# Moving the pair copies of q and k one slot ahead of their transposes, and software-pipelining the first unit, in a block-sparse attention kernel with a gated feed-forward layer

## The chip, the cores and the metric

The kernel runs on one core of one Trainium2 chip. The metric is the device time of one execution in microseconds (us), lower is better. Every run is marked fast or slow by its granted TensorE clock and its time; one single execution of this study was slow and is left out of all comparisons (it is shown, because it is odd).

Words used below: **PE** is TensorE, **DVE** is VectorE, **ACT** is ScalarE, **POOL** is GpSimd, whose queue issues the input loads. A **unit** is 256 query rows of one batch (12 units: 4 batches of 3). A main-loop unit has six **slots** of two steps; slots 1 and 2 carry output-layer products of an earlier unit ("output slots"), slots 3 to 6 carry gate and value products ("gated slots").

## The reference, cut to what matters

```python
scores = (1/sqrt(D)) * q @ k.T                  # B=4, H=8, S=768, D=64, float32
scores = where(mask, scores, -1e9)              # block mask of 32x32 blocks
attn = softmax(scores); x = attn @ v
x = x.transpose(0, 2, 1, 3).reshape(B*S, H*D)   # 3072 x 512
out = ((sigmoid(x @ w_gate) * (x @ w_val)) @ w_out).astype(float32)   # 512 -> 1536 -> 512
```

## The kernel before

q, k and v are loaded as float16 with the rows on partitions. A pair of heads is prepared by a DVE copy that lays the two heads side by side (`pr`), PE transposes into PSUM (`tpq`), and a copy into `qT` or `kT`:

```python
def prep(src, dst, b, p, t0=0, t1=NT, eng=None):
    pr = work.tile([128, NT, 2, D], f16, tag="pr", bufs=3, name="pr")
    nc.vector.tensor_copy(pr[:, t0:t1, :, :], src[b % 2][...])          # cut
    tp = ps.tile([128, 1024], f16, tag="m", bufs=4, name="tpq")
    for t in range(t0, t1):
        nc.tensor.transpose(tp[:, ...], pr[:, t, :, :], ident)          # cut
    # copy tp to dst[b % 2][:, p, ...] on nc.vector, or nc.scalar if asked

def vcopy(b, p): ...          # DVE: v16 -> vex (v with a column of ones), one pair

class Step:                   # one pair of heads, two key tiles, 256 queries
    def qk(self): ...         # PE: 4 matmuls -> st (PSUM, 2 buffers)
    def exp(self): ...        # ACT: pt = exp(st / 8), 128 x 1024
    def mul(self): ...        # DVE: pt *= mask
```

In the first unit each step runs to its end before the next begins; in the main loop one preparation stands at the end of a slot:

```python
for p in range(NP):                              # first unit
    for j in range(3):
        st = steps[p][j]
        st.qk(); st.exp()
        # ... build mask tiles ...
        st.mul()
        if p + 1 < NP:
            if j == 0: prep(k16, kT, 0, p + 1)
            if j == 1: prep(q16, qT, 0, p + 1, 0, 2)
        # ... xts, vcopy, value, rest of q ...

for n in range(1, len(units)):                   # main loop
    for sl in range(6):
        sa.qk(); sb.qk()                         # sb later in two slots of unit 2
        sa.exp(); sa.mul()
        F.f(fs[0])                               # gated slot; F.y(...) in an output slot
        sb.exp(); sb.mul()
        if sl % 3 in (0, 2): value()             # PV and normalisation of an earlier pair
        F.f(fs[1]); F.f(fs[2])
        if sl % 3 in (0, 1): xts()
        extra()      # one of: prep of k, prep of q, vcopy, for the next batch
```

`F.f` is 8 matmuls into `pg`, a tanh on ACT (`th`) and a product on DVE (`ht`). Program order is the order on each engine.

The softmax here doesn't subtract the row's maximum and nothing guards it: scores larger than these inputs give would overflow.

## Time and profile before

| | before |
|---|---|
| median time (4 runs) | 368.56 us (368.24 to 369.45) |
| span of the profiled run | 367.5 us |
| first scores of unit 1 / of unit 2 | 8.0 / 47.35 us |
| unit without preparations (e.g. 190.86 to 213.94) | 23.1 us |
| two units with 8 preparations (132.65 to 190.86) | 58.2 us |

First the page of the profile: busy time by engine; then the span in 40 slices of 9.2 us (a digit is the busy share in tenths; PEclk is the granted TensorE clock; GB/s is what the transfers moved); then the chain of waits that ended last, by engine.

```profile
span 367.5 us, 8103 instructions
...
PE 311.2 (85%) x3470; PEld 221.2 (60%) x3470; DVE 225.0 (61%) x534; ACT 210.9 (57%) x320; POOL 25.9 (7%) x37
...
PE   2566457889879999888889999799889999999995
...
PEclk9999999999999999999999999999999999999999
...
GB/s 108 193 202 205 204 204 181 2 3 57 2 78 162 78 2 59 2 2 58 2 2 57 3 30 30 0 2 59 3 2 57 3 30 30 2 59 1 30 30 57
...
PE 79%; DVE 11%; ACT 6%; issue 2%; DMA 1%; DVEq 0%; ACTq 0%; POOLq 0%
...
```

PE is the bound: 85% busy and 79% of the chain. But its digits show a weak start (2 to 7 for seven slices) and dents afterwards. The GB/s row shows the input transfers running at about 204 GB/s until the seventh slice, that is until about 64 us.

The dents. The view of two stretches (length, then busy time of PE, its weight loads, DVE, ACT and POOL, each with the instruction count, then the granted clock, DMA share and GB/s):

```profile
...
132.65:190.86 58.21, 50.25 (x594) 36.64 (x594) 38.60 (x92) 34.43 (x52) 0.00 (x0) 1.00 0.05 20
190.86:213.94 23.08, 23.08 (x273) 16.97 (x272) 15.86 (x38) 17.00 (x26) 0.00 (x0) 1.00 0.07 24
...
```

In units without preparations PE never stops. In the two units with eight of them it is idle for 58.21 - 50.25 = 8.0 us. The tile view of `tpq` in this stretch gives just that: 8 waits for the copy `pr`, 8.0 us in total. One of them in order of time (start, duration, engine, line, operation, output <- input, count, and in brackets the engine's idle time before it and what ended it):

```profile
...
150.60 0.87 DVE L303 SCALAR_TENSOR_TENSOR ht<-th,pg 128x256 f16<-128x256 f32 x2
150.63 0.38 ACT L302 ACTIVATE th<-pg 128x256 f32<-128x256 f32 x1 [0.49 <-PE pg L292]
151.38 0.28 DVE L279 COPY xT<-tpx 128x256 f16<-128x256 f16 x1
151.58 0.35 DVE L188 COPY pr<-k 128x768 f16<-128x768 f16 x1
...
151.99 0.51 PE L194 MATMUL tpq<-ident,pr 128*128 128x128 f16 x6 [1.29 <-DVE pr L188]
...
152.43 0.61 PE L222 MATMUL st<-qT,kT 64*128 64x256 f16 x8
...
```

DVE works off its queue in order: the last two `ht` of the slot, then xT, then `pr`; the input of this copy was on chip since about 64 us, when the loads of the first three batches were done. The transposes wait 1.29 us for the copy, and the scores (L222), which need nothing of it, wait behind the transposes. This agrees with the Trainium skill, "TensorE: Matmul & The Clock Gate", the specification table, which calls DVE's queue a strict FIFO.

The first unit, one step in order of time:

```profile
...
29.11 0.69 DVE L236 TENSOR_TENSOR pt<-pt,mask 128x1024 f16<-128x1024 f16 x1 [0.71 <-ACT pt L232]
29.72 0.35 DVE L188 COPY pr<-k 128x768 f16<-128x768 f16 x1
...
30.13 0.82 PE L194 MATMUL tpq<-ident,pr 128*128 128x128 f16 x6 [1.91 <-DVE pr L188]
...
32.20 0.61 PE L222 MATMUL st<-qT,kT 64*128 64x256 f16 x4
...
32.85 1.02 ACT L232 ACTIVATE pt<-st 128x1024 f16<-128x1024 f32 x1 [3.29 <-PE st L222]
...
```

Product, copy, transposes (PE waited 1.91 us), PV, scores, exponential (ACT waited 3.29 us): one serial chain through three engines.

And the clock. The same eight score matmuls early and late:

```profile
...
57.18 1.04 PE L222 MATMUL st<-qT,kT 64*128 64x256 f16 x8
...
64.81 0.61 PE L222 MATMUL st<-qT,kT 64*128 64x256 f16 x8
...
```

Until 61.4 us every matmul of this run ran at half rate. The PEclk row prints 9 there because the trace has no clock record before that time; the durations decide. The Trainium skill, "TensorE: Matmul & The Clock Gate", Part 1, describes it: half clock until a busy window of about 3.4 us.

### The profile page before, as it was taken

How to read it: one execution, taken by the hardware profiler on the slowest of the kernel's cores; microseconds unless marked ns; L12 is line 12 of the kernel's file. 1: busy time of each engine (PE TensorE's matmuls, PEld its weight loads, DVE VectorE, ACT ScalarE, POOL GpSimd, SP SyncE). 2: the span in 40 equal slices, each digit the busy share in tenths (PEclk: the TensorE clock that was granted, in tenths of full speed). 3: DMA queues.
4: the chain of work that ended last, by engine and by line, in shares of the span. 5: the costliest groups of instructions: out<-in, count | busy, mean ns of one | idle time of the engine just before them, and what ended most of it. 6: DMA issues, size and time to landing. Idle time of an engine off the chain costs nothing.

```text
span 367.5 us, 8103 instructions
## 1 busy us (share of the span) xinstructions
PE 311.2 (85%) x3470; PEld 221.2 (60%) x3470; DVE 225.0 (61%) x534; ACT 210.9 (57%) x320; POOL 25.9 (7%) x37
## 2 busy tenths in 40 slices
PE   2566457889879999888889999799889999999995
PEld 1133235765756866665666866566666858768682
DVE  2654455765765776775775766765775766757340
ACT  2244433655646766655566856565657867768241
POOL 8832010000010000000000000000000000000000
PEclk9999999999999999999999999999999999999999
DMA  8999999001059401001001000001001000010001
GB/s 108 193 202 205 204 204 181 2 3 57 2 78 162 78 2 59 2 2 58 2 2 57 3 30 30 0 2 59 3 2 57 3 30 30 2 59 1 30 30 57
DMA packets 23215, 21.03 MB, mean 57 GB/s; under 512 B 2164, under 2 KB 20108, under 8 KB 23180
## 3 DMA queue, kind: packets, MB, share of 16 engines
q0 software_dynamic: 19472, 14.16, 26.1%
q1 hardware_dynamic: 3708, 6.37, 4.7%
q8 instruction: 27, 0.44, 0.5%
q14 instruction: 8, 0.07, 0.1%
HBM read 28.39 MB, written 6.29 MB: 94 GB/s over the span
## 4 chain that ended last, share of the span: by engine, by line
PE 79%; DVE 11%; ACT 6%; issue 2%; DMA 1%; DVEq 0%; ACTq 0%; POOLq 0%
PE pg L292 32%; PE py L320 17%; PE st L222 11%; PE pv L254 10%; PE tpq L194 5%; ACT pt L232 5%; DVE pt L236 3%; DVE pr L188 3%; DVE ht L303 2%; DVE xT L279 1%; PE tpx L276 1%; DMA k<-in_k_dram 1%; ACT th L302 1%; PE pm L170 0%; DVE mask L182 0%
## 5 line engine op out<-in xcount | busy, mean ns | idle before, releaser
L232 ACT ACTIVATE pt<-st 128x1024 f16<-128x1024 f32 x144 | 144.7, 1021 | 66.5 <-PE st L222 65.8
L236 DVE TENSOR_TENSOR pt<-pt,mask 128x1024 f16<-128x1024 f16 x144 | 99.7, 692 | 79.0 <-ACT pt L232 78.6
L292 PE MATMUL pg<-xT,wg 128*128 128x256 f16 x576 | 87.3, 274 | 0.0
L292 PE MATMUL pg<-xT,wv 128*128 128x256 f16 x576 | 86.9, 274 | 0.0
L302 ACT ACTIVATE th<-pg 128x256 f32<-128x256 f32 x144 | 55.4, 385 | 44.0 <-PE pg L292 42.4
L320 PE MATMUL py<-wo,ht 128*128 128x512 f16 x288 | 67.7, 380 | 0.0
L303 DVE SCALAR_TENSOR_TENSOR ht<-th,pg 128x256 f16<-128x256 f32 x144 | 58.9, 416 | 11.1 <-ACT th L302 9.9
L194 PE MATMUL tpq<-ident,pr 128*128 128x128 f16 x192 | 19.8, 245 | 49.4 <-DVE pr L188 48.6
L292 PEld LDWEIGHTS <-wv 128*128 128x128 f16 x576 | 56.6, 98 | 6.7
L292 PEld LDWEIGHTS <-wg 128*128 128x128 f16 x576 | 50.7, 98 | 14.7 <-issue 8.2
L222 PE MATMUL st<-qT,kT 64*128 64x256 f16 x576 | 48.9, 288 | 0.5 <-ACT qT L199 0.5
L254 PEld LDWEIGHTS <-pt 128*128 128x128 f16 x1152 | 46.0, 102 | 4.6 <-issue 0.8
L254 PE MATMUL pv<-vex,pt 128*128 128x65 f16 x1152 | 48.0, 199 | 0.4 <-DVE pt L236 0.4
L194 PEld LDWEIGHTS <-pr 128*128 128x128 f16 x192 | 12.4, 107 | 58.7 <-DVE pr L188 57.6
L320 PEld LDWEIGHTS <-ht 128*128 128x128 f16 x288 | 25.8, 98 | 30.5 <-issue 4.2
L329 ACT ACTIVATE ysb<-py 128x512 f32<-128x512 f32 x24 | 14.3, 597 | 36.6 <-PE py L320 36.6
L222 PEld LDWEIGHTS <-kT 64*128 64x128 f16 x576 | 22.4, 96 | 14.0 <-issue 7.3
L266 DVE TENSOR_TENSOR x<-pv,rz 128x256 f16<-128x256 f32 x48 | 20.4, 424 | 1.7
L279 DVE COPY xT<-tpx 128x256 f16<-128x256 f16 x48 | 13.8, 287 | 11.7 <-PE tpx L276 11.7
L201 DVE COPY qT<-tpq 128x768 f16<-128x768 f16 (+2 forms) x19 | 9.3, 488 | 11.5 <-PE tpq L194 11.5
L201 DVE COPY kT<-tpq 128x768 f16<-128x768 f16 x16 | 8.9, 558 | 11.2 <-PE tpq L194 11.2
L276 PE MATMUL tpx<-ident,x 128*128 128x128 f16 x96 | 13.7, 226 | 1.6 <-DVE x L266 1.5
(29 smaller groups left out, 79.7 us busy)
## 6 DMA issues: line engine op xcount, KB each, us to landing
out_dram<-ysb SPq DMA_DIRECT2D x24, 256.0 KB, 2.0
k<-in_k_dram POOLq DMA_DIRECT2D x3, 768.0 KB, 19.0
q<-in_q_dram POOLq DMA_DIRECT2D x3, 768.0 KB, 9.1
v<-in_v_dram POOLq DMA_DIRECT2D x3, 768.0 KB, 11.5
wg<-in_moe_w_gate_dram POOLq DMA_DIRECT2D x4, 384.0 KB, 12.2
wv<-in_moe_w_val_dram POOLq DMA_DIRECT2D x4, 384.0 KB, 13.4
wo<-in_moe_w_out_dram POOLq DMA_DIRECT2D x3, 512.0 KB, 16.6
k<-in_k_dram POOLq DMA_DIRECT2D x4, 192.0 KB, 6.3
```

What stands on the lines that cost most here:

```text
L194: nc.tensor.transpose(tp[:, (t - t0) * 128 : (t - t0 + 1) * 128], pr[:, t, :, :], ident)
L201: nc.vector.tensor_copy(d_, tp[:, 0 : (t1 - t0) * 128])
L222: nc.tensor.matmul(self.st[:, a, i, :], kT[b % 2][o : o + D, p, t * 128 : (t + 1) * 128], qT[b % 2][o : o + D, p, u * UQ : (u + 1) * UQ], ...
L232: nc.scalar.activation(self.pt, self.st, AF.Exp, bias=0.0, scale=SCALE)
L236: nc.vector.tensor_tensor(self.pt, self.pt, m.unsqueeze(1).broadcast_to([128, 2, 2, UQ]), op=ALU.mult,)
L254: nc.tensor.matmul(self.acc[:, s, a, :], self.steps[t // 2].pt[:, a, t % 2, s * 128 : (s + 1) * 128], vex[self.b % 2][:, 2 * self.p + a, t ...
L266: nc.vector.tensor_tensor(self.x16, self.acc[:, :, :, 0:D], rz.broadcast_to([128, 2, 2, D]), op=ALU.mult,)
L279: nc.vector.tensor_copy(self.xT[:, self.p, :], tp[:, 0:UQ])
L292: nc.tensor.matmul(self.pg[:, i, :], w[:, c, f * 128 : (f + 1) * 128], self.xT[:, c, :], start=(c == 0), stop=(c == 3),)
L302: nc.scalar.activation(th, self.pg[:, 0, :], AF.Tanh, bias=0.0, scale=0.5)
L303: nc.vector.scalar_tensor_tensor(self.ht[:, f, :], in0=th, scalar=1.0, in1=self.pg[:, 1, :], op0=ALU.add, op1=ALU.mult,)
L320: nc.tensor.matmul(self.py, self.ht[:, f, s * 128 : (s + 1) * 128], wo[:, f, :], start=(f == 0), stop=(f == NF - 1),)
```

## The change

Its intent: let other work of PE stand between a pair's copy and its transposes, and run the first unit as a software pipeline, so that scores, exponentials, mask products and the next pair's transposes overlap. The core of the diff:

```diff
-    def prep(src, dst, b, p, t0=0, t1=NT, eng=None):
-        pr = work.tile([128, NT, 2, D], f16, tag="pr", bufs=3, name="pr")
+    def pair_copy(src, b, p, t0=0, t1=NT):
+        pr = work.tile([128, NT, 2, D], f16, tag="pr", bufs=4, name="pr")
         nc.vector.tensor_copy(...)
+        return pr
+    def pair_turn(pr, dst, b, p, t0=0, t1=NT, eng=None):
         tp = ps.tile(...)            # transposes and copy out, as before
...
-    def extra():
-        if todo: todo.popleft()()
+    def extra_pe():
+        if copied:
+            pr, dst, b, p, t0, t1 = copied.popleft()
+            pair_turn(pr, dst, b, p, t0, t1)
+            if dst is qT and t0 == 0:
+                vcopy(b, p)
+    def extra_copy():
+        if pairs:
+            src, dst, b, p, t0, t1 = pairs.popleft()
+            copied.append((pair_copy(src, b, p, t0, t1), dst, b, p, t0, t1))
...          # first unit, s = 0 .. 11, p, j = s // 3, s % 3:
+        if j == 0 and p + 1 < NP:
+            pair_turn(prk, kT, 0, p + 1)
+            prq = pair_copy(q16, 0, p + 1, 0, 2)
+        if s > 0: flat[s - 1].mul()
+        if s + 1 < 12: flat[s + 1].exp()
+        if j == 1 and p + 1 < NP:
+            pair_turn(prq, qT, 0, p + 1, 0, 2, nc.scalar)
+        if s + 2 < 12: flat[s + 2].qk()
...          # mask tiles, vcopy, value, xts, rest of q, cut
...          # main loop:
             sa.exp()
+            extra_pe()
             sa.mul()
...
                 xts()
-            extra()
+            extra_copy()
```

The arithmetic stays the same. The V copy no longer has a slot of its own: it follows the transposes of q in the same slot. So the eight preparations of a batch take eight slots in a row instead of eight of twelve. The new first unit bundles more than the pipeline: q's copy out of PSUM moves from DVE to ACT for the later pairs (`nc.scalar` above), and the mask tiles are built in another order.

More of the change, by code (lines that the diff above doesn't have):

```diff
@@ L335, in y @@
                 )
-    todo = deque()
-    def extra():
-        if todo:
-            todo.popleft()()
+    pairs = deque()
+    copied = deque()
+    def extra_pe():
[8 more added lines that the diff above has]
+            copied.append((pair_copy(src, b, p, t0, t1), dst, b, p, t0, t1))
     units = [(b, u) for b in range(B) for u in range(NU)]
@@ L357, in begin @@
             for p in range(NP):
-                todo.append(lambda b=b, p=p: prep(k16, kT, b + 1, p))
-                todo.append(lambda b=b, p=p: prep(q16, qT, b + 1, p))
-                todo.append(lambda b=b, p=p: vcopy(b + 1, p))
+                for src, dst in ((k16, kT), (q16, qT)):
+                    pairs.append((src, dst, b + 1, p, 0, NT))
         return [[Step(b, u, p, j) for j in range(3)] for p in range(NP)]
@@ L375 @@
     steps = begin(0)
-    prep(k16, kT, 0, 0)
-    prep(q16, qT, 0, 0, 0, 2, nc.scalar)
-    mask_blocks()
-    for p in range(NP):
-        for j in range(3):
-            st = steps[p][j]
-            st.qk()
-            st.exp()
-            if p == 0 and j == 0:
-                mask_rows()
-            if p == 0:
-                mask_tile(0, UQ, 2 * j, nc.vector)
-            if 1 <= p <= 2:
-                mask_tile(UQ, S, 3 * (p - 1) + j, nc.scalar)
-            st.mul()
-            if p + 1 < NP:
-                if j == 0:
-                    prep(k16, kT, 0, p + 1)
-                if j == 1:
-                    prep(q16, qT, 0, p + 1, 0, 2)
-            if j == 1:
-                xts()
-            if j == 0:
-                vcopy(0, p)
-                value()
-            if p == NP - 1:
-                prep(q16, qT, 0, j, 2, NT)
-        waiting.append(Pair(*units[0], p, steps[p], xTs[0]))
@@ L404 @@
-    todo.append(lambda: prep(q16, qT, 0, 3, 2, NT))
+    flat = [st for p in range(NP) for st in steps[p]]
+    pr = pair_copy(k16, 0, 0)
+    pair_turn(pr, kT, 0, 0)
+    pr = pair_copy(q16, 0, 0, 0, 2)
+    pair_turn(pr, qT, 0, 0, 0, 2, nc.scalar)
+    mask_blocks()
+    flat[0].qk()
+    flat[0].exp()
+    flat[1].qk()
+    mask_rows()
+    prk = pair_copy(k16, 0, 1)
+    mask_tile(0, UQ, 0, nc.vector)
+    prq = None
+    for s in range(12):
+        p, j = s // 3, s % 3
+        if j == 0 and p + 1 < NP:
+            pair_turn(prk, kT, 0, p + 1)
+            prq = pair_copy(q16, 0, p + 1, 0, 2)
+        if s > 0:
+            flat[s - 1].mul()
+        if s + 1 < 12:
+            flat[s + 1].exp()
+        if j == 1 and p + 1 < NP:
+            pair_turn(prq, qT, 0, p + 1, 0, 2, nc.scalar)
+        if s + 2 < 12:
+            flat[s + 2].qk()
+        if p == 0 and j < 2:
+            mask_tile(0, UQ, 2 * j + 2, nc.vector)
+        if j == 0:
+            vcopy(0, p)
+        if s >= 4 and j == 1:
+            value()
+        if s >= 6 and j == 0:
+            xts()
+        if j == 2 and p + 2 < NP:
+            prk = pair_copy(k16, 0, p + 2)
+        if 3 <= s < 9:
+            mask_tile(UQ, S, s - 3, nc.scalar)
+        if s >= 8:
+            extra_pe()
+        if 7 <= s:
+            extra_copy()
+        if s == 6:
+            for i in range(NP):
+                pairs.append((q16, qT, 0, i, 2, NT))
+        if j == 2:
+            waiting.append(Pair(*units[0], p, steps[p], xTs[0]))
@@ L406 @@
+    flat[11].mul()
+    extra_pe()
     for n in range(1, len(units)):
@@ L415 @@
             sa.exp()
+            extra_pe()
             sa.mul()
@@ L441 @@
                 xts()
-            extra()
+            extra_copy()
             for p, j in pair:
```

## The prediction

> **What bounds the kernel now.** Tensor work, plus waits at the pair copies. The chain of waits is 79% PE, 11% VectorE, 6% ScalarE. From the timeline (starts of each slot's scores):
>
> - Units without transposes of q and k take 23.1 us; those with them (second and third of a batch) 29.1 us. Per batch that is 8 preparations: 8 x 0.44 us of transposes and about 8.0 us in which PE waits for the copy `pr` (0.65 us behind slots of output work, 1.2 to 1.4 us behind gated slots, where the copy stands behind the last `ht` on VectorE). The tile view of `tpq` gives 24.2 us of such waits after 64 us.
> - The first unit runs from 7.5 to 47.35 us, a serial chain of score, exponential, mask product, pair copy, transpose; PE waits 21.3 us for `pr` in it. I estimate about 25 us of work for each engine there.
> - Until 61.4 us every matmul runs at half rate: 8 score matmuls take 1.04 us, later 0.61. This agrees with the Trainium skill, "TensorE: Matmul & The Clock Gate", Part 1 (half clock until a busy window of about 3.4 us; here PE is continuously busy from 58.15 us).
> - Input transfers run at about 204 GB/s until 64 us. From issue and time to landing, k of batch 1 lands at about 45.6, q at 49.4, v at 53.3 us.
>
> **What the change does.** Work stays the same. (a) Main loop: the copy still ends a slot, but its transposes stand behind the next slot's eight score matmuls, so 0.54 us of PE work fills the wait. VectorE is first in, first out (same page, the specification table), and the copy still waits for the last `ht`; so the wait shrinks, not vanishes: 1.2 to 1.4 becomes 0.7 to 0.85, 0.65 becomes 0.1. (b) The V copy (0.35 us) moves ahead of a mask product; the second exponential, behind the tanh, hides it. (c) The first unit issues scores two steps ahead, products one step late.
>
> **On the critical path.**
> - Batches 2 and 3: waits 8.0 to about 3.4 us each; saves about 9.7 together.
> - Batch 1 after the third slot of the second unit: about 6 us (one preparation less there, waits from about 8.2 to 3.1).
> - First unit: my hand schedule ends it at about 39 us instead of 47.4. But the second unit then meets the transfers: the k copy waits for 45.6, q for 49.4, and the V copy, now inside the third slot ahead of the mask product, for 53.3. So of 8.4 us about 6.3 remain at the end of that slot. This gate also forgives some error in my schedule.
>
> Sum 22 us: 368.5 to about 347 us, range 342 to 353. Chance of faster by over 2%: 0.95; within 2%: 0.04; slower by over 2%: 0.01.
>
> **What would show it.** Second unit's first score at 37 to 42 us; VectorE idle before the copies of k, q and v of batch 1, released by DMA; units with transposes at about 26.6 us instead of 29.1; PE waits for `pr` after 64 us falling from 24 to about 10 us; units without transposes unchanged at 23.1 us; full PE clock from about 54 us.
>
> **What would make it wrong.** PE reaching full clock much earlier in the denser first unit (faster, though the transfers cap it); VectorE, with the extra V copy, becoming the limit in gated slots (saves less); in-order waits in the first unit, such as the normalisation behind PV behind the ScalarE transpose copy, holding it beyond 43 us; batch 1 landing later than now.

## The result, and the profile after

| | before | after |
|---|---|---|
| median (4 runs each) | 368.56 us | 344.62 us (344.28 to 344.92) |
| ratio, 95% interval | | 0.9346, 0.9327 to 0.9366 |
| span of the profiled run | 367.5 us | 343.1 us |
| first scores of unit 2 | 47.35 us | 36.54 us |
| two units with 8 preparations | 58.2 us | 52.7 us |
| unit without preparations | 23.1 us | 23.1 us |

A ratio here is the mean time of one kernel's fast runs over the mean of the other's of the same rounds, so it is not quite the ratio of the medians. The same lines of the page of the kernel after:

```profile
span 343.1 us, 8102 instructions
...
PE 308.3 (90%) x3470; PEld 221.2 (64%) x3470; DVE 220.4 (64%) x531; ACT 210.3 (61%) x323; POOL 26.0 (8%) x37
...
PE   2788459899999999899999998999999999999995
...
GB/s 98 187 202 204 206 204 204 88 3 172 168 31 32 3 31 32 2 32 33 0 32 33 2 61 2 2 32 33 0 60 6 2 61 2 31 34 3 61 2 61
...
PE 76%; DMA 12%; DVE 6%; ACT 2%; POOL 2%; issue 1%; POOLq 0%
...
```

PE is 90% busy. Its row stands at 7 and 8 through the first unit (second to fourth slice of 8.6 us each), then drops to 4 and 5 for two slices, in which the transfers still run at 206 and 204 GB/s. DMA has appeared in the chain of waits with 12%: it held 1% before. The two stretches that correspond to those shown of before:

```profile
...
119.23:171.97 52.74, 49.39 (x593) 36.62 (x593) 38.30 (x93) 34.00 (x52) 0.00 (x0) 1.00 0.06 21
171.97:195.06 23.09, 23.09 (x273) 16.98 (x273) 15.59 (x37) 17.00 (x26) 0.00 (x0) 1.00 0.07 25
...
```

PE's idle time in the two units with preparations is 52.74 - 49.39 = 3.35 us, from 8.0 us; the unit without them is unchanged. (PE's busy time fell by 0.86 us as well, although the matmuls are the same. A likely reason, not tested: the record of a matmul of 256 columns is some 274 ns long while the next one starts about 110 ns after it, so each stop of PE may let one such overhang show as busy time, and there are fewer stops.) The tile view of `tpq` counts four waits for `pr` in this stretch, 2.9 us in total, where it counted eight. One preparation in order of time:

```profile
...
136.94 0.86 DVE L306 SCALAR_TENSOR_TENSOR ht<-th,pg 128x256 f16<-128x256 f32 x2
136.97 0.38 ACT L305 ACTIVATE th<-pg 128x256 f32<-128x256 f32 x1 [0.49 <-PE pg L295]
...
136.98 0.61 PE L225 MATMUL st<-qT,kT 64*128 64x256 f16 x8
...
137.73 0.28 DVE L282 COPY xT<-tpx 128x256 f16<-128x256 f16 x1
137.93 0.35 DVE L188 COPY pr<-q 128x768 f16<-128x768 f16 x1
...
138.33 0.51 PE L197 MATMUL tpq<-ident,pr 128*128 128x128 f16 x6 [0.74 <-DVE pr L188]
```

The DVE order is the same: `ht`, `ht`, xT, `pr`. But PE has run the scores (136.98 to 137.59) meanwhile, so its wait is 0.74 us instead of 1.29.

The second unit, where the chain now runs through the transfers:

```profile
...
45.56 0.36 DVE L188 COPY pr<-k 128x768 f16<-128x768 f16 x1 [5.17 <-DMA k<-in_k_dram]
...
45.97 0.82 PE L197 MATMUL tpq<-ident,pr 128*128 128x128 f16 x6 [6.19 <-DVE pr L188]
...
49.45 0.36 DVE L188 COPY pr<-q 128x768 f16<-128x768 f16 x1
...
49.87 0.82 PE L197 MATMUL tpq<-ident,pr 128*128 128x128 f16 x6 [0.80 <-DVE pr L188]
...
53.28 0.37 DVE L207 COPY vex<-v 128x768 f16<-128x768 f16 x1 [1.99 <-DMA v<-in_v_dram]
...
```

The copy of k of batch 1 stood 5.17 us on its load, and PE 6.19 us on the copy. The chain of waits in order of time names the load of q that follows (start, duration, what):

```profile
...
28.55 20.88 DMA q<-in_q_dram
...
49.45 0.37 DVE pr L188
...
49.87 0.82 PE tpq L197 x6
...
```

Where the 24.4 us of span came from, by the same event in both traces: the last gate product of unit 2's third slot ends at 63.16 us before and 55.99 us after, so **7.2 us** were won by there. Unit 4 begins at 109.55 and 96.14 us: 13.4 us, so **6.2 us** more in the rest of batch 1's preparations. Batches 2 and 3 give 58.2 - 52.7 = **5.5 us** each. Nothing changes after that.

### The profile page after: what moved, and what is told of

Its sections match the earlier page's. It is cut to its first block, busy times and chain, and to the rows that moved or that the text cites. A ratio compares the mean times of both kernels' runs of the same rounds, so it can differ in the third digit from the quotient of the medians.

```text
span 343.1 us, 8102 instructions
## 1 busy us (share of the span) xinstructions
PE 308.3 (90%) x3470; PEld 221.2 (64%) x3470; DVE 220.4 (64%) x531; ACT 210.3 (61%) x323; POOL 26.0 (8%) x37
## 4 chain that ended last, share of the span: by engine, by line
PE 76%; DMA 12%; DVE 6%; ACT 2%; POOL 2%; issue 1%; POOLq 0%
PE pg L295 36%; PE py L323 18%; PE pv L257 10%; PE st L225 6%; DMA q<-in_q_dram 6%; DMA wg<-in_moe_w_gate_dram 4%; PE tpq L197 3%; DVE pr L188 2%; DMA k<-in_k_dram 2%; DVE ht L306 2%; PE tpx L279 1%; DVE xT L282 1%; ACT pt L235 1%; ACT th L305 1%; DVE pt L239 1%
## 5 line engine op out<-in xcount | busy, mean ns | idle before, releaser
L306 DVE SCALAR_TENSOR_TENSOR ht<-th,pg 128x256 f16<-128x256 f32 x144 | 59.0, 416 | 10.8 <-ACT th L305 9.0
L295 PEld LDWEIGHTS <-wg 128*128 128x128 f16 x576 | 51.5, 98 | 11.4 <-issue 4.4
L257 PEld LDWEIGHTS <-pt 128*128 128x128 f16 x1152 | 45.6, 101 | 4.7 <-issue 1.0
L197 PE MATMUL tpq<-ident,pr 128*128 128x128 f16 x192 | 19.7, 244 | 25.6 <-DVE pr L188 23.5
L279 PEld LDWEIGHTS <-x 128*128 128x128 f16 x96 | 9.1, 99 | 7.1 <-issue 1.2
```

What stands on the lines that cost most here:

```text
L197: nc.tensor.transpose(tp[:, (t - t0) * 128 : (t - t0 + 1) * 128], pr[:, t, :, :], ident)
L257: nc.tensor.matmul(self.acc[:, s, a, :], self.steps[t // 2].pt[:, a, t % 2, s * 128 : (s + 1) * 128], vex[self.b % 2][:, 2 * self.p + a, t ...
L279: nc.tensor.transpose(tp[:, s * 128 : (s + 1) * 128], self.x16[:, s, :, :], ident)
L295: nc.tensor.matmul(self.pg[:, i, :], w[:, c, f * 128 : (f + 1) * 128], self.xT[:, c, :], start=(c == 0), stop=(c == 3),)
L306: nc.vector.scalar_tensor_tensor(self.ht[:, f, :], in0=th, scalar=1.0, in1=self.pg[:, 1, :], op0=ALU.add, op1=ALU.mult,)
```

## The experiments

All are timed against the kernel before on the same chip. All twelve runs gave the correct result. Theory: (a) the main loop gains because score work fills the wait for the copy, and what remains of that wait is the copy's place in DVE's order; (b) the first unit gains more than the time shows, because the input transfers hold the second unit. Rivals are named with each run.

### 1 and 2: each half of the change alone

`e1_first_unit_only`: new first unit, old main loop.

```diff
             sa.exp()
-            extra_pe()
             sa.mul()
...
-            extra_copy()
+            if todo: todo.popleft()()    # copy+transposes of k / of q / vcopy, as before
```

> New first unit, old main loop (copy and transposes together at the end of the slot, V copy in its own slot). My theory: the first unit's gain reaches the third slot of the second unit only as the 7.1 us that the loads of batch 1 let through, plus about 2 us because the preparations of batch 1 begin one slot earlier: 359 to 361 us. PE waits for the pair copies after 64 us stay near 23 us. Rival: the whole 10.8 us by which the second unit starts earlier is worth its full size: 357.5 or less.

Measured: 360.93 us, ratio 0.9794 (0.977 to 0.9818). PE waited 21.3 us for `pr` after 64 us.

`e2_main_loop_only`: the first unit is the code of before, the main loop is new (diff: the loop over `s` replaced by the old two loops).

> Old first unit, new main loop. My theory: 5.5 us each for batches 2 and 3 and about 6 us for batch 1, so 350 to 353 us, units with transposes at 26.4 us on average, second unit's first score still at 47.3 us. Rival (the first unit carries most of the gain): 357 us or more.

Measured: 350.88 us, ratio 0.9517 (0.9495 to 0.9538).

So the main loop brings 17.8 us and the first unit 7.8 us; their sum, 25.6 us, is about 1.5 us more than the whole change, probably because both let the preparations of batch 1 start or end earlier (not tested). The gain of e1 alone is about 2%, but its interval is clear of no change. In e1 unit 2 began at 36.6 us, 10.8 us earlier than before, but only 7.8 us arrived at the end: the rival with the full size falls.

### 3: is it the score work, or the distance of one slot?

```diff
             sa, sb = (steps[p][j] for p, j in pair)
+            extra_pe()
             sa.qk()
...
             sa.exp()
-            extra_pe()
             sa.mul()
```

> The change with one move: the transposes of the copied pair stand ahead of the next slot's scores, the copy still ends the slot before. My theory (the gain of the main loop is the score work that fills the wait): the waits return, 0.54 to 0.65 us at each of about 24 preparations, 356 to 359 us. Rival (giving the copy a slot of its own is what helps): 344 to 346 us.

Measured: 360.32 us, ratio 0.9774 (0.9755 to 0.9793), the time of e1 within 0.6 us. It came out 1.3 us above the range that I had given. The same two units:

```profile
...
123.90:181.80 57.90, 50.21 (x593) 36.63 (x592) 38.84 (x93) 34.55 (x52) 0.00 (x0) 1.00 0.05 19
...
```

57.9 us, against 52.7 after and 58.2 before; the waits for `pr` in this stretch are 7.7 us again. The copy still stood a slot ahead by its name, but a copy at the end of one slot and transposes at the start of the next are neighbours in time. The rival falls: nearly all of the main loop's gain in this stretch (5.2 of 5.5 us) is the eight score matmuls put between them. This run keeps the fourth `pr` buffer and the new place of the V copy, so neither of these is the cause.

### 4: the copy earlier in DVE's order

```diff
             sb.mul()
+            if sl >= 2: extra_copy()
             if sl % 3 in (0, 2): value()
...
-            extra_copy()
+            if sl < 2: extra_copy()
```

> The change, and in gated slots the copy goes right behind the slot's second mask product, ahead of the last two gate products, instead of behind them. My theory: the remaining waits of 0.66 to 0.85 us (12 of them, 8.7 us) go, since only the place of the copy in VectorE's order causes them: 335 to 338 us. Rival (VectorE is by now as long as PE in gated slots): the later gate products hold PE instead and the time stays at 342 us or more.

Measured: 335.07 us, ratio 0.9093 (0.9071 to 0.9116), 9.5 us faster than the change. The same stretch, then one preparation:

```profile
...
115.60:165.20 49.60, 49.16 (x593) 36.62 (x592) 37.79 (x93) 34.02 (x52) 0.00 (x0) 1.00 0.06 23
...
```

```profile
...
132.04 0.35 DVE L188 COPY pr<-q 128x768 f16<-128x768 f16 x1
...
132.63 0.61 PE L225 MATMUL st<-qT,kT 64*128 64x256 f16 x8
132.86 0.74 DVE L306 SCALAR_TENSOR_TENSOR ht<-th,pg 128x256 f16<-128x256 f32 x2
...
133.17 0.51 PE L197 MATMUL tpq<-ident,pr 128*128 128x128 f16 x6
...
```

The copy is done at 132.39 us, before the slot's last `ht`, and the transposes at 133.17 follow the scores without a wait. PE's idle time for `pr` in the stretch is zero; 49.6 us is what two units without preparations (2 x 23.1) and eight times 0.44 us of transposes add up to (49.7). DVE was not the limit.

### 5, 6 and 7: what holds the second unit

`e5_wo_late` issues the loads of the output weights behind those of batch 1; `e6_before_wo_late` does the same to the kernel before, as a control.

```diff
-    for j in range(3):
-        load_wo(j)
...
             for src, dst in ((k, k16), (q, q16), (v, v16)):
                 load_heads(dst, src, b + 1, 0, H)
+        if n == 0:
+            for j in range(3):
+                load_wo(j)
```

> The change, with the loads of the output weights issued behind those of batch 1 instead of ahead of them; 1.5 MB less ahead of batch 1 is about 7.6 us at 200 GB/s, so k of batch 1 lands at about 38, q at 42, v at 46 us. My theory (transfers hold the second unit): PE's wait of 6.2 us for the k copy goes, 338 to 340 us. Rival (half clock or VectorE holds the second unit as well): under 2 us gained, 343 us or more.

> Control: the same order of loads in the kernel before, whose second unit asks for batch 1 only after it has landed. My theory: no gain, 367.5 to 369.5 us. Rival (the order helps whatever the first unit does): 363 us or less.

Measured: e5 339.38 us, ratio 0.9202 (0.9181 to 0.9223), 5.2 us faster than the change; e6 369.03 us, ratio 1.0004 (0.9981 to 1.0028). In e5 the copies and transposes of k and q of batch 1 in unit 2:

```profile
...
40.83 0.35 DVE L186 COPY pr<-k 128x768 f16<-128x768 f16 x1
...
41.24 0.51 PE L195 MATMUL tpq<-ident,pr 128*128 128x128 f16 x6 [1.16 <-DVE pr L186]
...
44.38 0.82 PE L195 MATMUL tpq<-ident,pr 128*128 128x128 f16 x6 [0.80 <-DVE pr L186]
...
```

The copy starts at 40.83 us instead of 45.56, with no wait for its load. So the transfers did hold the second unit of the changed kernel, and they did not hold that of the kernel before, which came too late to meet them.

`e7_v_late` tests a step of my prediction, the gate at 53.3 us by the load of v:

```diff
             if dst is qT and t0 == 0:
-                vcopy(b, p)
+                vlate.append((b, p))
...
             extra_copy()
+            if vlate: vcopy(*vlate.popleft())
```

> The change, with the V copy at the end of the slot of its q transposes instead of ahead of that slot's first mask product. My prediction held that the wait for v at 53.3 us gates the third slot of the second unit; the chain of the kernel after does not show v on it. If the prediction's step holds: 1 to 2 us faster, 342.5 to 343.5. If the chain is right: within 0.5 us of 344.6, or a little slower, as the V copy then delays the pair copy behind it... it stands after the pair copy, so no delay is expected.

Measured: 344.96 us, ratio 0.9354 (0.9332 to 0.9377), against 0.9346 of the change: no gain. DVE no longer waits for v:

```profile
...
56.67 0.36 DVE L207 COPY vex<-v 128x768 f16<-128x768 f16 x1
...
```

Yet nothing is won: the wait of 1.99 us at 53.28 us was real and hidden. This run also puts the V copy's general place, ahead of a mask product, at no cost: the same two units take 52.76 us here (118.84 to 171.60), against 52.74.

### 8: both remedies together

The diffs of e4 and e5 together.

> Copy behind the second mask product and output weights loaded late, together. If the two causes are independent, the gains add: 8.7 and 5.5 us off 344.6, so 329 to 332 us. If they share something, 333 us or more.

Measured: 329.44 us, ratio 0.894 (0.8916 to 0.8964), 15.2 us less than the change; 9.5 + 5.2 = 14.7. The gains add up within 0.5 us, so the two causes are independent as far as this shows.

### 9 to 12: the first unit, with both remedies in

With the transfers out of the way, the first unit's own waits are on the chain. e9 moves one line, e10 adds throw-away matmuls while PE waits for the first load, e11 does both, and e12 is e9 once more.

```diff
# e9
+        if j == 1 and p + 1 < NP:
+            pair_turn(prq, qT, 0, p + 1, 0, 2, nc.scalar)
         if s + 1 < 12:
             flat[s + 1].exp()
-        if j == 1 and p + 1 < NP:
-            pair_turn(prq, qT, 0, p + 1, 0, 2, nc.scalar)
# e10
+    nc.vector.memset(hot, 1.0)           # hot: 128 x 512, f16; ph: a PSUM tile nobody reads
+    for i in range(9):
+        nc.tensor.matmul(ph, hot[:, 0:128], hot, start=True, stop=True)
```

> Early copy and late output weights as in the run before, and in the first unit ScalarE's copy of the transposed q goes ahead of the exponential of the next step instead of behind it. In the trace PE waits 1.54 us for that copy twice and 0.52 us once before the scores, and the chain then runs through PV and the normalisation. Theory (ScalarE's order holds PE there): about 0.9 us less at each of two places, 327 to 328.5 us. Rival (the chain moves to the exponential, which is now 0.37 us later): 329 us or more.

> Early copy and late output weights, and nine throw-away matmuls of 512 columns while PE waits for the first load. If the half clock is set by PE being idle, full clock comes by about 8 us, and if the first unit (PE busy about 75%) holds it, about 15 us of half-clock matmuls on the chain shrink: 323 to 327 us. If the clock falls back within one or two windows of about 3.4 us, or never rises because the nine matmuls do not fill a window: 328.5 to 330.5 us.

> Both together. If the clock holds: 320 to 326 us, with the order on ScalarE worth at least as much as alone. If the clock falls back: as without the throw-away matmuls, 327 to 329 us.

> The kernel with early copy, late output weights and the ScalarE copy ahead of the exponential once more, because its profiled run fell at a granted clock of 0.68 (441 us) and left no profile to compare. Expected: 327 to 328.5 us at full clock, PE waits for the ScalarE copy of q down from 4.1 us to about 2. If 441 us belongs to the kernel and not to the chip's state at that moment, some of the runs are that long again.

Measured: e9 328.39 us median of all five executions (328.06 us of the four fast ones), ratio of fast runs 0.8898 (0.8879 to 0.8916); e12 327.95 us, ratio 0.89 (0.8889 to 0.8911); e10 329.75 us, ratio 0.8936 (0.8908 to 0.8963); e11 327.58 us, ratio 0.8895 (0.8879 to 0.8911).

The line moved in e9 is worth about 1.5 us: e12's interval lies just below e8's (they ran on different chips, each against the kernel before). PE's wait for the ACT copy of q, in the table of who waited for whom (total us, times, longest), first of e8, then of e12:

```profile
...
PE st L223 <- ACT qT L200: 4.1, 4, 1.5
...
```

```profile
...
PE st L223 <- ACT qT L200: 2.2, 4, 0.6
...
```

The throw-away matmuls did not pay. In the profiled run of e10 full clock came at 4.2 us, lasted 6.8 us and fell back, and that execution took 327.15 us; the other four, 329.19 to 330.26 us, are no faster than e8. In the profiled run of e11 the clock did not rise before 38 us at all. How often the warm start took can be read from the mean granted clock for every execution, in which the time before the first clock record counts as full: a clock that rises early and falls back shows as a lower mean. The profiled execution of e10 has 0.952 and three of the other four 0.948; three of e11's five have 0.948 to 0.958; no fast execution without the throw-away matmuls is below 0.973. So the warm start probably took in four executions of e10, and three of these took 329.19 to 330.17 us. What is shown is that full clock does not hold through the first unit.

One execution of e9 took 441.11 us, with DVE and ACT as fast as ever but PE slow throughout. A stretch of it:

```profile
...
120.00:160.00 40.00, 40.00 (x350) 26.11 (x348) 22.67 (x54) 20.16 (x31) 0.00 (x0) 0.65 0.04 15
...
```

The granted clock was 0.65 for the whole main part. The other four runs of e9 and all six of e12, the same kernel on the same chip, were fast, so this is a state of the chip and not of the kernel. Its cause is open.

## Why the prediction was right or wrong

The time, 344.62 us, lies in the predicted range of 342 to 353 us, 2.4 us below the value of 347. The predicted sum of 22 us was made of 9.7, 6 and 6.3; the spans give 10.9, 6.2 and 7.2. Step by step:

- **Main loop, filled wait: right.** Predicted 1.2 to 1.4 becoming 0.7 to 0.85 us and 0.65 becoming 0.1; measured 0.66 to 0.85 us and zero. e3 shows the cause, e4 shows what the rest was.
- **Batches 2 and 3: mechanism right, term too small.** "saves about 9.7 together" measured 10.9 us (58.2 to 52.7, twice). The wait behind output slots vanished instead of leaving 0.1 us, four times a batch: the waits for `pr` fell from 8.0 to 2.9 us. The stretch shrank by 0.4 us more than the waits did; why, no run shows.
- **Rest of batch 1: right.** Predicted about 6, measured 6.2 us.
- **First unit's end: somewhat pessimistic.** Predicted about 39 us (37 to 42 as the test), measured 36.54, just outside the test. The prediction's reading of the first unit was loose: its 21.3 us of waits for `pr` include the 5.52 us before the very first transposes, so 15.8 us fall between 7.5 and 47.35 us; and its estimate of 25 us of work for each engine is far too high for ACT (from 5 to 47 us PE was busy for 23.46, DVE for 23.21, ACT for 15.33 us). The error hardly reached the time, because the load of k then held the second unit, as the prediction had said.
- **The gate of the transfers: right for k and q, wrong for v.** The k copy ran at 45.56 us (predicted 45.6), the q copy at 49.45 (49.4), the V copy at 53.28 (53.3). For q this is partly chance: the work that follows the k copy kept DVE until about 49.3 us, so the load of q held it for only 0.1 us more. And the step "the V copy, now inside the third slot ahead of the mask product, for 53.3" as part of the limit failed: e7 took that wait away and gained nothing. From the q copy on, PE's own work is the limit, at half clock: transposes, 8 matmuls of gate and value products, and PV fill it until 53.72 us, and DVE has made up for v by then: before the slot's last `ht`, at 56.45 us, it was idle for 0.40 us waiting for ACT. So 7.2 us of the earlier start remained instead of 6.3. e5 and e6 show that the transfers are the cause of the loss.
- **The clock: right in time, incomplete.** Predicted full clock from about 54 us; it came at 54.7. I had not foreseen an earlier window at full clock in the denser first unit. Three stretches of the kernel after:

```profile
...
34.20:37.60 3.40, 1.90 (x33) 1.25 (x30) 3.37 (x10) 0.89 (x2) 1.15 (x2) 1.00 1.25 206
37.60:54.60 17.00, 9.61 (x90) 6.52 (x91) 6.84 (x17) 5.57 (x7) 0.60 (x1) 0.50 1.30 204
54.70:64.00 9.30, 7.90 (x101) 6.49 (x100) 6.97 (x19) 4.91 (x9) 0.00 (x0) 1.00 1.26 196
...
```

It lasted 3.4 us, in which PE was busy for 1.90 us, and fell back to one half at 37.6 us, 2.2 us before PE ran into the wait for k (39.78 us). It is not a property of the denser first unit either: the profiled runs of e3, e4, e5 and e7 have the same first unit and no full clock before their second unit, which begins at 36.85 to 37.02 us, while those of the change and of e1 had the early window and begin it at 36.54 and 36.60 us. So the window was worth 0.3 to 0.5 us of the 2.5 us by which the first unit beat my schedule; the rest is the schedule's own error.
- **PE waits for `pr` after 64 us.** Predicted from 24 to about 10 us; measured 7.3 us. The fixed border flatters this: two more waits behind gated slots (0.66 and 0.74 us) now fall before 64 us, and all twelve add up to 8.7 us.

What would have been better foreseen: the change was treated as a given, and two reorderings of a few lines next to it (e4 and e5), both readable from the profile of before, are worth 15 us more. The fastest version without throw-away matmuls, e12, takes 327.95 us, against 344.62 us of the change (e11, with them, takes 327.58 us, the same within the intervals).

## What to carry to other kernels

A producer placed "one slot ahead" of its consumer is only as far ahead as the work that stands between them on both engines: put independent work of the waiting engine between, and put the producer ahead of whatever its own in-order queue makes it wait for (here 9.5 us from moving one copy up). When a start-up phase is shortened, ask which loads the next phase will then meet, and order the loads by the time of first use; the same reorder is worth nothing before (e6) and 5.2 us after (e5). A wait that a profile shows is worth something only if it is on the chain: the wait for v was 2 us long and cost none.

## What the Trainium skill lacked or had wrong

- "TensorE: Matmul & The Clock Gate", Part 1, puts the ramp penalty at under 1% of a typical kernel's span. That figure should not be carried over to a start-up phase in which PE keeps waiting: here the half clock lasted until 61.4 us of a 367.5 us span before, and until 54.7 us of 343.1 us after but for one window of 3.4 us. PE was 56% busy from 5 to 47 us before (23.46 of 42 us) and never left half clock. What the half clock cost in time was not measured.
- The same part reports a granted ratio of one half or one, a limit of 13/16 for dies with three busy cores and, as a state seen to stick, one quarter. A run of this one-core program (e9's profiled one) was granted 0.65 from 47.7 us on and took 441.11 instead of about 328 us; no page lists this value.
- The same page says that the full clock comes after a busy window and that frequent short idles of PE can make it swing between half and full. Its figure for losing it is an idle window of about 3.4 us, and it gives no share of use. Here it was lost with far shorter gaps: after the warm start of e10 it lasted 6.8 us, with PE busy for 62% (4.21 of 6.80 us) and no gap over 0.8 us; in the kernel after it lasted 3.4 us, with PE busy for 56% (1.90 of 3.40 us) and a longest gap of 1.29 us.
